# Attention in front of two expert layers: pooled v taken from 32-row blocks on TensorE, sums of outputs at the head of an iteration

## The chip, the core and the metric

The kernel runs on one core of a Trainium2 chip. TensorE (PE in the rows, its weight loads PEld) does the matmuls, VectorE (DVE), ScalarE (ACT) and GpSimd (POOL) the element work, SyncE (SP) issues the DMAs. The metric is the time of one execution on the device in microseconds (us).

## What is computed

Three layers stand behind each other: an attention, a dense layer with a gated activation, and a mixture of experts. The change touches the attention alone (batch 4, 8 heads, 576 positions, head size 64). It adds two attentions: one over positions that are averaged in fours, repeated back to full length, and a local one in which each position sees those less than four away.

```python
q_d = q.reshape(B, H, Sd, factor, D).mean(axis=3)      # factor = 4, Sd = 144
k_d = k.reshape(B, H, Sd, factor, D).mean(axis=3)
v_d = v.reshape(B, H, Sd, factor, D).mean(axis=3)
out_up = np.repeat(sm_attn(q_d, k_d, v_d), factor, axis=2)
mask = np.abs(pos[:, None] - pos[None, :]) < factor
scores = np.where(mask, scale * np.matmul(q, k.transpose(0, 1, 3, 2)), -1e9)
attn = np.exp(scores - max);  attn = attn / (sum(attn) + 1e-09)
return out_up + np.matmul(attn, v)                     # sm_attn has the same softmax
```

## The kernel before

**Units.** The attention works in 16 units u of two heads: four batches b of four pairs of heads (NP = 4). A half batch j (four heads) is loaded at once: k and q in `load_a` (tiles kn, qn, and rm for the last 64 rows). v is loaded twice. `load_v(b, n)` brings a quarter of batch b for the local attention into vw[b % 2]: 32-row blocks that overlap by eight, six blocks to a quarter, 24 to a batch, each block one DMA of 64 KB in runs of 256 bytes, for all eight heads. `load_v4(j, c)` brings the same values a second time for the pooled attention: 288 KB in runs of 1 KB, 16 such loads, which `pool_v` adds up in fours on GpSimd into vp.

**The loop.** Iteration `it` of 20 runs a pipeline over the units, each engine in program order: `transposes(it+1)` on TensorE, `copies(it+1)` and `p_copies(it+1)` on ScalarE (they bring k and q, transposed, from PSUM into SBUF), `normalize(it-1)` and `p_normalize(it-1)` (sums and reciprocals on VectorE, products on GpSimd), `merge(it-3)` (VectorE adds pooled and local outputs, SP stores them), `scores(it)` and `p_scores(it)` on TensorE, `relay(it+2)` (ScalarE and VectorE reorder k and q), `load_a`, `outputs(it-2)` on TensorE, `softmax(it)` and `p_softmax(it)` (maxima on VectorE, exponentials on ScalarE), `scatter(it-1)`, `p_transposes(it-1)`, `pt_copies(it-1)`, and then the pooling of the next half batch on GpSimd and the loads of v. Between them `prep_step` puts pieces of the preparation of the dense layer's weights (DVE lines 204, 209, 214, 219, ACT lines 195 and 199), one or two of them an iteration at first, three from iteration 5 on.

**What sets the order.** All loads go through SP's one queue in program order. Eight semaphores are used for them in turn, so that from the ninth DMA on each waits until the one eight places ahead of it has landed. PSUM has eight banks that `bank()` hands out in turn: ten to an iteration, so that each use waits for the readers of the use eight before it. The last five iterations also hold the first matmuls of the dense layer (L711). With iteration 16 the attention's own loads are over; behind the attention the program is a dense and an expert layer.

The lines of before that the steps need: transposes L381 to L383, copies L392 to L405, scores L413 and L418, pooled scores L453, softmax L426 to L428, pooled softmax L462 and L464, sums L434 to L437 and L469 to L471, scatter L443 and L447, pooled transposes and copies L479 and L486, outputs L499 to L506, merge L518, v loads L330 and L340, v pooling L354 and L355.

## Time and profile before

| | us |
|---|---|
| median of 3 runs (lowest, highest) | 845.87 (843.55, 846.75) |
| the profiled execution | 849.41 |
| its span | 847.7 |

| engine | busy us of the span |
|---|---|
| PE | 761.4 (90%) |
| DVE | 593.6 (70%) |
| ACT | 526.9 (62%) |
| POOL | 220.3 (26%) |

The span is the profiled execution without what lies around it (1.7 us). The busy shares are means over stages with different limits. From about 164 us on PE is busy for 635.97 of the 684.10 us left; the attention, which the change touches, lies ahead of that, and there no engine is busy all the time. The stretches below are cut at the starts of the mask matmul (L413) of an iteration: iteration 2 starts at 24.07, 3 at 41.37, 7 at 70.57, 14 at 129.06 us.

### The profile page before, as it was taken

What the parts mean: (1) busy time and instruction counts of PE and PEld (TensorE: products, weight loads), DVE (VectorE), ACT (ScalarE), POOL (GpSimd) and SP (SyncE); (2) the same over time, 40 slices, a digit from 0 to 9 for tenths busy, and PEclk for the clock granted to TensorE, in tenths of its full rate; (3) what the DMA queues carried; (4) which work ended last, traced back from release to release, by engine and by line L of the source; (5) the groups of instructions that cost most, each with busy time, mean ns of one, the idle gap of its engine ahead of it and who ended that gap; (6) DMA issues with size and microseconds to landing.
All of it is one profiled execution on the core that took longest, in us unless ns stands there. A gap on an engine that the chain in (4) does not pass through costs nothing. (4 is left out here: it accounts for less than half of the span.)

```text
span 847.7 us, 14454 instructions
## 1 busy us (share of the span) xinstructions
PE 761.4 (90%) x5078; PEld 644.4 (76%) x5078; DVE 593.6 (70%) x1414; ACT 526.9 (62%) x1019; POOL 220.3 (26%) x212
## 2 busy tenths in 40 slices
PE   5597786799979999999999899899789999999991
PEld 4475665588858888888899788789688887899981
DVE  6499998689966874388439658968766555666652
ACT  6597886899846556655666567554336554565551
POOL 7577673100000000000000110337323232332330
PEclk9699988999979999999999999999999999999996
DMA  7999991455623110010001004546577667767762
GB/s 171 221 185 217 233 239 62 142 149 180 192 66 127 63 26 0 14 57 20 0 13 58 20 29 183 76 39 197 103 223 222 208 194 235 223 228 240 199 213 63
DMA packets 90066, 112.99 MB, mean 133 GB/s; under 512 B 39915, under 2 KB 62077, under 8 KB 89725
## 3 DMA queue, kind: packets, MB, share of 16 engines
q1 hardware_dynamic: 85421, 101.35, 44.7%
q0 software_dynamic: 4560, 10.60, 3.6%
q8 instruction: 42, 0.69, 0.4%
q14 instruction: 43, 0.35, 0.2%
HBM read 97.06 MB, written 15.12 MB: 132 GB/s over the span
## 5 line engine op out<-in xcount | busy, mean ns | idle before, releaser
L731 DVE TENSOR_TENSOR t<-bk,t 128x512 f32<-128x512 f32 (+1 forms) x80 | 50.0, 633 | 100.8 <-ACT t L725 100.8
L678 POOL DMA_INDIRECT ids_by_expert<-tok_id,g_pi x18 | 20.8, 1154 | 279.1 <-DVE run L677 104.3
L638 DVE SCALAR_TENSOR_TENSOR junk<-o,wgb 128x512 f32<-128x512 f32 x120 | 85.0, 708 | 2.9
L719 ACT ACTIVATE t<-bk 128x512 f32<-128x512 f32 (+1 forms) x80 | 44.0, 550 | 54.5 <-PE bk L711 52.8
L740 DVE TENSOR_TENSOR gg<-t,gg 128x512 fp32r<-128x512 f32 (+1 forms) x80 | 57.3, 720 | 7.5 <-ACT gg L729 4.2
L729 ACT CAST gg<-t 128x512 fp32r<-128x512 f32 (+1 forms) x57 | 32.7, 573 | 40.0 <-DVE t L731 33.7
L711 PE MATMUL bk<-x,wi0h 128*128 128x512 f32 (+1 forms) x160 | 52.3, 407 | 5.4 <-DVE x L699 5.1
L720 ACT ACTIVATE t<-t,half 128x512 f32<-128x512 f32 (+1 forms) x80 | 54.6, 682 | 2.6
L1097 POOL DMA_INDIRECT out_dram<-yo,oid x19 | 25.4, 1338 | 115.7 <-ACT yo L1096 69.2
L1083 ACT ACTIVATE hT<-bk 128x256 fp32r<-128x256 f32 x80 | 30.4, 383 | 35.6 <-PE bk L1081 33.1
L725 ACT ACTIVATE t<-t,hpi 128x512 f32<-128x512 f32 (+1 forms) x80 | 52.2, 674 | 0.2
L711 PE MATMUL bk<-x,wi1h 128*128 128x512 f32 (+1 forms) x160 | 47.8, 381 | 4.2 <-DVE t L731 4.2
L751 PE MATMUL bk<-wo1h,gg 128*128 128x512 f32 x144 | 48.3, 406 | 0.0
L1084 DVE SCALAR_TENSOR_TENSOR hT<-bk,hT 128x256 fp32r<-128x256 f32 x80 | 32.9, 420 | 21.5 <-ACT hT L1083 21.4
L711 PE MATMUL bk<-x,wi3h 128*128 128x512 f32 (+1 forms) x160 | 46.9, 375 | 0.6 <-DVE rank L673 0.6
L711 PE MATMUL bk<-x,wi2h 128*128 128x512 f32 (+1 forms) x160 | 46.1, 369 | 0.0
L751 PE MATMUL bk<-wo3h,gg 128*128 128x512 f32 x144 | 46.1, 392 | 0.0
L751 PE MATMUL bk<-wo0h,gg 128*128 128x512 f32 x144 | 45.9, 393 | 0.0
L751 PE MATMUL bk<-wo2h,gg 128*128 128x512 f32 x144 | 45.8, 392 | 0.0
L711 PEld LDWEIGHTS bk<-x,wi0h 128*128 128x128 f32 x160 | 31.9, 204 | 13.6 <-DVE x L699 7.0
L711 PEld LDWEIGHTS bk<-x,wi1h 128*128 128x128 f32 x160 | 30.6, 195 | 8.9 <-DVE t L731 4.6
L1081 PE MATMUL bk<-x,ew10h 128*128 128x256 f32 x160 | 31.8, 288 | 5.7 <-DVE x L1016 2.4
(308 smaller groups left out, 2338.2 us busy)
## 6 DMA issues: line engine op xcount, KB each, us to landing
est<-in_moe_w_dram SPq DMA_DIRECT2D x88, 512.0 KB
wst<-in_moe_w_in_dram SPq DMA_DIRECT2D x16, 512.0 KB
wst<-in_moe_w_out_dram SPq DMA_DIRECT2D x16, 512.0 KB
vw<-in_v_dram SPq DMA_DIRECT2D x88, 64.0 KB
v<-in_v_dram SPq DMA_DIRECT2D x16, 288.0 KB
x_second<-o SPq DMA_DIRECT2D x18, 256.0 KB
kn<-in_k_dram SPq DMA_DIRECT2D x8, 512.0 KB
qn<-in_q_dram SPq DMA_DIRECT2D x8, 512.0 KB
```

The costliest lines, as they stand in the source:

```text
L638: V.scalar_tensor_tensor(wgb["junk"], x2[tl], 1.0, wgb[e], op0=ALU.mult, op1=ALU.mult, accum_out=gate[tl][:, e:e + 1])
L711: PE.matmul(h, a[:, f % QF, kk], x[:, c], start=n == 0, stop=n == 3 * KD - 1)
L719: A.activation(t, bk[f % GF][:, :BLK[j]], AF.Tanh, scale=0.5)
L720: A.activation(t, t, AF.Arctan, scale=-0.5, bias=half)
L725: A.activation(t, t, AF.Sin, scale=-2.0, bias=hpi)
L729: A.copy(gg[:, 0], t_)
L731: V.tensor_tensor(t, bk[f % GF][:, :BLK[j]], t, op=ALU.mult)
L740: V.tensor_tensor(gg[:, 1], t, gg[:, 0], op=ALU.subtract)
L751: PE.matmul(acc[t], gg[:, a, c], w[:, f % QF], start=f == 0 and n == 0, stop=f == NF - 1 and n == 2)
L1081: PE.matmul(ps[:, :256], W1(i, a, kk, f), xt[i][:, c, kk], start=n == 0, stop=n == 3 * KD - 1)
L1083: A.activation(hT[:, 0, f], ps[:, :256], AF.Relu)
L1084: V.scalar_tensor_tensor(hT[:, 1, f], ps[:, :256], 0.0, hT[:, 0, f], op0=ALU.max, op1=ALU.subtract)
```

## The change

**Pooled v.** `load_v4` and `pool_v` go. `pool_vw(b)` takes the sums from the 32-row blocks: a matrix pool_v (128 x 32, built once) with ones where a row belongs to a group of four; six matmuls of 512 columns for a batch write 32 PSUM rows each, at one of four column places of the array, into two banks; two ScalarE copies bring them to vp. This stands at the end of iterations 1, 5, 9 and 13. The 32-row layout leaves eight idle rows in each 32, so the pooled probabilities `pe` get the same layout, with zeros between (two tiles that GpSimd clears once), and their transposes and products have 128 and 64 rows in place of 72 and 72.

**Loads.** All four quarters of the first batch are loaded ahead of the loop, ahead of `load_a(2)`, which stood between the second and the third quarter. Of each later batch two quarters are loaded in iteration 4b+1, one each in the next two; before, one in each of four iterations.

**The order.** `merge(it-3)` moves from behind the sums to the head of the iteration.

**Constants.** The exponentials e get a 33rd column that holds 1e-9, so that one sum (L434) gives the denominator and L435 goes. The scaling and constant of the pooled sums moves from VectorE (L469) to ScalarE, behind the exponentials.

```diff
+    KP = (128, 32 * (T - 4))
+        es = [ac.tile([128, 2 * T, W + 1], F32, name=f"e{i}") for i in range(2)]
+        pool_v = ac.tile([128, W], F32, name="pool_v")
+        pes = [ac.tile([128, LQ, T, W], F32, name=f"pe{i}") for i in range(2)]
...
+            for t in es:
+                V.memset(t[:, :, W:], 1e-9)
...
-            for t in pbd:
+            for t in pbd + pes:
                 G.memset(t, 0.0)
...
-        def pool_v(j, c):
-            v4 = bt[j]["v4", c]
-            vp = wk.tile([HS, HB, D], F32, tag="vp", name="vp", bufs=6)
-            G.tensor_tensor(v4[:, :, 0:2], v4[:, :, 0:2], v4[:, :, 2:4], op=ALU.add)
-            G.tensor_tensor(vp, v4[:, :, 0], v4[:, :, 1], op=ALU.add)
-            bt[j]["vp", c] = vp
+        def pool_vw(b):
+
+            ps = [bank(f"pv{c}") for c in range(2)]
+            for t in range(T):
+                c, i = divmod(t, 4)
+                PE.matmul(ps[c][32 * i:32 * i + 32], pool_v, vw[b % 2][:, t], tile_position=(0, 32 * i))
+            vp = wk.tile([128, 2, H * D], F32, tag="vp", name="vp", bufs=1)
+            for c in range(2):
+                A.copy(vp[:KP[c], c], ps[c][:KP[c]])
+            st["v"] = vp
...
-            V.tensor_reduce(sm, e, axis=X, op=ALU.add)
-            V.tensor_scalar(sm, sm, 1e-9, None, op0=ALU.add)
+            V.tensor_reduce(sm, es[u % 2], axis=X, op=ALU.add)
...
-                A.activation(pe[:, g], p3[:, g], AF.Exp, bias=pm[:, g:g + 1], accum_out=pz[:, g:g + 1])
+                A.activation(pe[:, g, :, :QB], p3[:, g].rearrange("p (t a) -> p t a", t=T), AF.Exp, bias=pm[:, g:g + 1], accum_out=pz[:, g:g + 1])
+            A.activation(pz, pz, AF.Copy, scale=4.0, bias=4e-9)
...
-            V.tensor_scalar(pz, pz, 1e-9, 4.0, op0=ALU.add, op1=ALU.mult)
             V.reciprocal(pz, pz)
...
-        for c in range(2):
-            load_v4(0, c)
-        for n in range(NP - 1):
+        for n in range(NP):
             load_v(0, n)
-            if n == LA:
-                load_a(2)
+        load_a(2)
         setup_p()
...
-        pool_v(0, 0)
-        load_v4(1, 0)
...
+            if 3 <= it < U + 3:
+                merge(it - 3)
             if it + 1 < U:
                 transposes(it + 1)
...
-            if 3 <= it < U + 3:
-                merge(it - 3)
...
-            m, odd = divmod(it + 1, 2)
-            b, n = divmod(it + NP - 1, NP)
-            if b < B:
-                load_v(b, n)
-            if m < NH:
-                pool_v(m, odd)
-            if m + 1 < NH:
-                load_v4(m + 1, odd)
+            b, n = divmod(it, NP)
+            if n == 1 and b < B:
+                pool_vw(b)
+            if n and b + 1 < B:
+                for z in ((), (0, 1), (2,), (3,))[n]:
+                    load_v(b + 1, z)
```

**SP's queue ahead of the loop.** vw_169 is the buffer of batch 0, v_267 and v_269 are the second copy of v. Before:

```order
L330 DMA v_267<-in_v_dram 72x4x256
L330 DMA v_269<-in_v_dram 72x4x256
L340 DMA vw_169<-in_v_dram 28x8x64
L340 DMA vw_169<-in_v_dram 32x8x64 x11
L323 DMA kn<-in_k_dram 128x4x256
L324 DMA rm<-in_k_dram 64x4x64
L323 DMA qn<-in_q_dram 128x4x256
L324 DMA rm<-in_q_dram 64x4x64
L340 DMA vw_169<-in_v_dram 32x8x64 x6
```

and now:

```order
L344 DMA vw_169<-in_v_dram 28x8x64
L344 DMA vw_169<-in_v_dram 32x8x64 x22
L344 DMA vw_169<-in_v_dram 28x8x64
L333 DMA kn<-in_k_dram 128x4x256
L334 DMA rm<-in_k_dram 64x4x64
L333 DMA qn<-in_q_dram 128x4x256
L334 DMA rm<-in_q_dram 64x4x64
```

All 24 blocks of batch 0 stand directly behind the first two half batches of k and q; the third half batch stands behind them.

**TensorE at the end of iteration 1 and in iteration 2.** Before, the pooled transposes of unit 0 (L479) are followed by the transposes of unit 3, and v is first read by the outputs of unit 0:

```order
L479 MATMUL bk_97<-ident,pe 72x128 x2
L479 MATMUL bk_97<-ident,pe 72x32
L381 MATMUL bk_90<-ident,rl 128x128 x4
L382 MATMUL bk_92<-ident,pl 128x128
L381 MATMUL bk_91<-ident,rl 128x128 x4
L382 MATMUL bk_92<-ident,pl 128x128
L383 MATMUL bk_92<-pool_id,rm 128x2x80
L413 LDWEIGHTS id_b
L413 MATMUL bk_93<-mask,id_b 128x384
L418 MATMUL bk_93<-spare_98,qT_165 32x64 x24
L453 MATMUL bk_94<-kp,qbd_167 128x144 x3
L499 MATMUL bk_95<-pp,vp 64x144 x4
```

and now:

```order
L487 MATMUL bk_97<-ident,pe_174 64x128 x2
L487 MATMUL bk_97<-ident,pe_174 64x32
L360 MATMUL bk_90<-vw_169,pool_v 32x512 x4
L360 MATMUL bk_91<-vw_169,pool_v 32x512 x2
L389 MATMUL bk_92<-ident,rl 128x128 x4
L390 MATMUL bk_94<-ident,pl 128x128
L389 MATMUL bk_93<-ident,rl 128x128 x4
```

The six matmuls read all blocks of v, and the transposes and scores of the next units are queued behind them.

**VectorE in an iteration** (the one that holds the first weight piece, L204). Before, the merge (L518) stands between the reciprocals and the relay:

```order
L434 TENSOR_REDUCE sm<-e 128x12
L435 TENSOR_SCALAR sm<-sm 128x12
L436 RECIPROCAL sm<-sm 128x12
L469 TENSOR_SCALAR pz<-pz 128x3
L470 RECIPROCAL pz<-pz 128x3
L518 TENSOR_TENSOR x<-bk_96,pos 128x288
L518 TENSOR_TENSOR x<-bk_97,pos 128x288
L360 TENSOR_REDUCE rl<-qn 128x512
L204 TENSOR_SCALAR wm<-wm 128x512
```

and now:

```order
L526 TENSOR_TENSOR x<-bk_92,pos 128x288
L526 TENSOR_TENSOR x<-bk_93,pos 128x288
L442 TENSOR_REDUCE sm<-e_171 128x12
L443 RECIPROCAL sm<-sm 128x12
L477 RECIPROCAL pz<-pz 128x3
L368 TENSOR_REDUCE rl<-qn 128x512
L203 TENSOR_SCALAR wm<-wm 128x512
```

Two small operations are gone, and only the relay still stands between the reciprocals, which start GpSimd's products, and the weight piece.

## Rows read from the trace of the kernel before

**Rows 1.** Busy time of each engine in stretches; last PEclk, DMA share, GB/s.
```profile
24.07:41.37 17.30, 9.16 (x108) 6.75 (x105) 7.75 (x22) 8.76 (x27) 10.43 (x12) 0.65 1.12 230
41.37:70.57 29.20, 26.60 (x421) 21.12 (x420) 24.57 (x60) 26.67 (x89) 21.46 (x23) 0.92 0.96 197
70.57:129.06 58.49, 48.04 (x737) 37.84 (x735) 57.14 (x106) 50.06 (x160) 40.50 (x41) 0.91 0.96 224
129.06:163.60 34.54, 28.31 (x306) 21.59 (x303) 28.59 (x62) 23.71 (x61) 9.25 (x14) 0.90 0.29 97
```

**Rows 2.** Timeline, TensorE's outputs: start, us, instruction, idle before, releaser.
```profile
31.07 0.59 PE L504 MATMUL bk<-spare,vw 128*64 128x96 f32 x4 [3.79 <-DMA vw<-in_v_dram]
...
36.60 0.59 PE L504 MATMUL bk<-spare,vw 128*64 128x96 f32 x4 [0.93 <-DMA vw<-in_v_dram]
...
66.43 0.43 PE L504 MATMUL bk<-spare,vw 128*64 128x96 f32 x4 [2.05 <-DMA vw<-in_v_dram]
```

**Rows 3.** Timeline, ScalarE: first copy of units 3, 4 and 5.
```profile
25.33 0.58 ACT L392 COPY spare<-bk 64x512 f32<-64x512 f32 x1
...
39.80 0.58 ACT L392 COPY spare<-bk 64x512 f32<-64x512 f32 x1 [0.65 <-PE bk L381]
...
47.88 0.58 ACT L392 COPY spare<-bk 64x512 f32<-64x512 f32 x1
```

**Rows 4.** Timeline, SP's queue: issues of v, from the start on.
```profile
6.61 1.88 SPq L330 DMA_DIRECT2D v<-in_v_dram  x2
8.60 12.19 SPq L340 DMA_DIRECT2D vw<-in_v_dram  x12
...
23.35 3.06 SPq L340 DMA_DIRECT2D vw<-in_v_dram  x6
...
28.46 3.86 SPq L340 DMA_DIRECT2D vw<-in_v_dram  x6
```

**Rows 5.** Timeline, GpSimd: pooling of v.
```profile
15.44 1.26 POOL L354 TENSOR_TENSOR v<-v 72x512 f32<-72x512 f32 x1 [1.64 <-DMA v<-in_v_dram]
16.78 0.73 POOL L355 TENSOR_TENSOR vp<-v 72x256 f32<-72x256 f32 x1
```

**Rows 6.** Timeline: prices of small-tile and full fp32 matmuls, a 512-column copy, a small ScalarE operation.
```profile
18.60 0.88 PE L418 MATMUL bk<-spare,qT 128*32 128x64 f32 x48
...
19.41 1.00 PE L453 MATMUL bk<-kp,qbd 128*128 128x144 f32 x6
...
49.29 0.59 ACT L394 COPY qT<-bk 128x512 f32<-128x512 f32 x1
...
17.60 0.19 ACT L464 ACTIVATION_READ_ACCUMULATOR pe<-bk,pm 128x1 f32 x1
```

**Rows 7.** Groups of instructions from 70.57 to 129.06: count, busy, mean ns, idle before.
```profile
L428 ACT ACTIVATE e<-e 128x384 f32<-128x384 f32 x7 | 3.7, 524 | 6.3 <-DVE e L427 6.3
...
L469 DVE TENSOR_SCALAR pz<-pz 128x3 f32<-128x3 f32 x6 | 2.9, 481 | 0.0
...
L435 DVE TENSOR_SCALAR sm<-sm 128x12 f32<-128x12 f32 x6 | 1.5, 242 | 0.2
```

**Rows 8.** Timeline: weight pieces on VectorE beside GpSimd's products.
```profile
97.63 2.51 DVE L204 TENSOR_SCALAR wm<-wm 128x512 int32<-128x512 int32 x1
...
143.06 0.68 DVE L209 SCALAR_TENSOR_TENSOR wm<-wst,wm 128x512 int32<-128x512 int32 x1
...
143.12 1.39 POOL L471 TENSOR_TENSOR pe<-pe,pz 128x432 f32<-128x432 f32 x1
...
150.57 0.42 DVE L204 TENSOR_SCALAR wm<-wm 128x512 int32<-128x512 int32 x1
```

**Rows 9.** Timeline of iteration 15: the merge, and the outputs that wait for its bank.
```profile
141.16 0.55 DVE L434 TENSOR_REDUCE sm<-e 128x12 f32<-128x384 f32 x1
...
142.33 0.81 DVE L518 TENSOR_TENSOR x<-bk,pos 128x288 f32<-128x288 f32 x2
...
142.84 1.23 PE L504 MATMUL bk<-spare,vw 128*64 128x96 f32 x12 [4.83 <-DVE x L518]
```

More of the change, by code (lines that the diff above doesn't have):

```diff
@@ L158, in moe_kernel @@
     LAG = 5
-    LA = 1
     SC_A = (0, 1)
@@ L285, in setup_a @@
             V.tensor_copy(pool_id[:, :, RP:], ident[:2 * CR, :2 * CR].rearrange("p (z r) -> p z r", z=2))
+            V.memset(pool_v, 0.0)
+            V.tensor_reduce(
+                pool_v[:, :QB].rearrange("p (i a) -> p i a", i=4),
+                ident.rearrange("p (i w) -> p i w", i=4)[:, :, 4:4 + QB].rearrange("p i (a f) -> p i a f", f=4),
+                axis=X, op=ALU.add,
+            )
+            for t in es:
+                V.memset(t[:, :, W:], 1e-9)
             V.tensor_copy(id_b, ident)
@@ L325, in load_a @@
             bt[j] = {"n": (kn, qn), "rm": rm}
-        def load_v4(j, c):
-            b, h0 = j // 2, j % 2 * HB
-            v4 = ld.tile([HS, HB, 4, D], F32, tag="v4", name="v4")
-            SP.dma_start(out=v4.rearrange("p h r d -> p h (r d)"), in_=v[b, h0:h0 + HB, c * 4 * HS:(c + 1) * 4 * HS, :].rearrange("h (p r) d -> p h (r d)", r=4))
-            bt[j]["v4", c] = v4
         def load_v(b, n):
@@ L422, in softmax @@
             sc = st.pop(("s", u))
-            e = wk.tile(gsh, F32, tag="e", name="e")
+            e = es[u % 2][:, :, :W]
             mx = wk.tile([128, 2 * T], F32, tag="mx", name="mx")
@@ L442, in scatter @@
             et = wk.tile(gsh, F32, tag="et", name="et", bufs=1)
-            V.transpose(et.rearrange("p g q -> p (g q)"), e.rearrange("p g w -> p (g w)"))
+            V.transpose(et, e)
             pb = pbd[u % 2].rearrange("p t h i q -> p (t h) i q")
@@ L457, in p_softmax @@
             psc = st.pop(("ps", u))
-            pe = wk.tile([128, LQ, SPL], F32, tag="pe", name="pe")
+            pe = pes[u % 2]
             pm = wk.tile([128, LQ], F32, tag="pm", name="pm")
@@ L468, in p_normalize @@
             pe, pz = st["p", u]
-            V.tensor_scalar(pz, pz, 1e-9, 4.0, op0=ALU.add, op1=ALU.mult)
             V.reciprocal(pz, pz)
-            G.tensor_tensor(pe, pe, pz.unsqueeze(2).to_broadcast([128, LQ, SPL]), op=ALU.mult)
+            p4 = pe[:, :, :, :QB]
+            G.tensor_tensor(p4, p4, pz.unsqueeze(2).unsqueeze(3).to_broadcast([128, LQ, T, QB]), op=ALU.mult)
         def p_transposes(u):
@@ L483, in pt_copies @@
             tps = st[("q", u)]
-            pp = wk.tile([HS, 2, 2 * SPL], F32, tag="pp", name="pp", bufs=1)
+            pp = wk.tile([128, 2, 2 * SPL], F32, tag="pp", name="pp", bufs=1)
             for c in range(2):
-                A.copy(pp[:, c], tps[c][:HS, :2 * SPL])
+                A.copy(pp[:KP[c], c], tps[c][:KP[c], :2 * SPL])
             st["q", u] = pp
@@ L491, in outputs @@
             b, pg = divmod(u, NP)
-            vp, w_ = [bt[j]["vp", c] for c in range(2)], vw[b % 2]
+            vp, w_ = st["v"], vw[b % 2]
             pp = st.pop(("q", u))
@@ L498, in outputs @@
                 for h in range(2):
-                    PE.matmul(po[64 * h:64 * h + 64], vp[c][:, 2 * p + h], pp[:, c, SPL * h:SPL * h + SPL], start=c == 0, stop=c == 1, tile_position=(0, 64 * h))
+                    PE.matmul(po[64 * h:64 * h + 64], vp[:KP[c], c, (2 * pg + h) * D:(2 * pg + h + 1) * D], pp[:KP[c], c, SPL * h:SPL * h + SPL], start=c == 0, stop=c == 1, tile_position=(0, 64 * h))
             o = [bank(f"xo{i}") for i in range(2)]
```

3 lines of the change are left out of this document (1 added, 2 removed).

## Prediction, made before the changed kernel was run

> **What bounds the kernel now.** I read the stretches first [rows 1], since the busy shares of the whole span mix stages. The change lies in the first 164 us; what follows is moved as a whole, so a gain there is a gain of the run. The four stretches have different limits. From 24.07 to 41.37, iteration 2, no engine is busy for more than 10.43 of 17.30 us, while the DMA engines are full: this is a wait for loads. The timeline says which: TensorE stands three times before the outputs of unit 0, until 36.60, for blocks of v [rows 2]. From 41.37 to 70.57 ScalarE is busy for 26.67 of 29.20 us over four iterations, 6.7 us for each: it sets the pace, but for one more wait for v, 2.05 us at 66.43 [rows 2]. From 70.57 to 129.06 VectorE is busy for 57.14 of 58.49 us, and ScalarE for 50.06; ScalarE's largest wait there, 6.3 us, is for VectorE [rows 1, 7]. From 129.06 on engines wait for each other in turn; the longest such wait is TensorE's 4.83 us before 142.84 for a bank that the merge must empty [rows 9]. A gain within 0.5% (4.2 us) could not be told from no change.
>
> **The start.** On ScalarE the copies of unit 3 begin at 25.33, of unit 5 at 47.88 [rows 3]: 22.6 us for two iterations that take 13.4 at ScalarE's own pace. So 9.2 us are lost there, to v and to what follows from it (TensorE's granted clock is 0.65 of full speed in that stretch [rows 1]). Now the second copy of v is gone and all 24 blocks stand together. Before, twelve were issued in 12.19 us from 8.60 on [rows 4]; the seventh had to wait for the first of the pooled-v loads, since it stands eight places behind it, and that load had landed only when GpSimd took it at 15.44 [rows 5]. Later blocks cost SP 0.51 to 0.64 us each (3.06 and 3.86 for six [rows 4]). With the first twelve out by about 16 (14.7 at 0.51 each, 20.8 as before), the other twelve at 0.55 and some 3 us to land (before, the last left SP at 32.3 and was used at 36.60, which bounds it at 4.3), v is complete at about 25.6, and at 23 to 31 by the bounds. TensorE now needs it at the end of iteration 1 and not in iteration 2. One matmul and one copy stand behind the last block, so ScalarE begins unit 3 at about 27.1, 1.8 late, and unit 5 two iterations of 6.9 later, at 40.9 in place of 47.88: 7.0 us. The third half batch of k and q is now issued behind v, which I charge with 1. **Gain 6**, bounds 2 and 8.
>
> **The pooled v.** Six fp32 matmuls of 512 columns are 3072 columns a batch. The nearest row in form, 24 matmuls of 64 columns at the same four column places of the array, takes 0.88 us for 1536 columns [rows 6]: 1.8 us a batch. Full-width fp32 matmuls take 1.00 us for three of 144 columns [rows 6]: 7.1 us a batch, the other end. I take 1.8. The Trainium skill (TensorE: Matmul & The Clock Gate, Why this matters for your kernels) gives 2.38 times for three column tiles with 512 columns; by that figure the six would take an estimated 3.0 us, and the run would be at most 4.8 us longer. The two copies are of 512 columns, 0.59 each [rows 6]: 1.2 us of ScalarE a batch. TensorE's 1.8 hides beside the copies of the unit before where ScalarE sets the pace; if that cover is gone it costs 1.8 for each of the three later batches. The 16 poolings on GpSimd, 1.26 and 0.73 [rows 5], were off the path: they go for nothing, and in their place the clearing of the two pe tiles at the start costs nothing.
>
> **ScalarE's small operation.** It is one more small operation a unit; the read-out of a sum takes 0.19 [rows 6], so 0.2. On VectorE it and L435 took 2.9 and 1.5 us in seven iterations [rows 7]. The 33rd column, the wider transposes and the constants cost nothing that I can see: the sums grow by 3%, the rest is covered.
>
> **From 41.37 to 70.57.** ScalarE's pace stays. The 2.05 of waiting goes, since a batch is complete about two iterations before it is read; four small operations (0.8) and one pair of copies (1.2) come. **Gain 0**, bounds 2 lost (TensorE's 1.8 uncovered) and 1 won.
>
> **From 70.57 to 129.06.** VectorE goes from 57.14 to 52.7; ScalarE from 50.06, with seven small operations and two pairs of copies, to 53.9. ScalarE is late next: with no waits the stretch would be 4.6 shorter. Two engines this close do not run without waits, and ScalarE has 2.1 us of others than those for VectorE already (58.49 less 50.06 and 6.3), so I leave 3. **Gain 1.7**, bounds 2 lost and 4.6 won.
>
> **From 129.06 on.** The sum and the reciprocals of unit 14, from 141.16 to 142.33, no longer stand ahead of the merge for which TensorE waits [rows 9]. **Gain 1.2**, bounds 0.5 and 2. Elsewhere, too, the merge frees its banks sooner; SP stores its result from the same place in its queue.
>
> **The sum.** 6 + 0 + 1.7 + 1.2 = 8.9 us. The profiled execution would go from 849.4 to 840.5; the median of the runs, 3.5 lower than it, from 845.9 to **837.0**.
>
> **The rivals.** *VectorE loses a cover.* The merge (0.81 [rows 9]) ran beside GpSimd's first product. Now the weight pieces come that much sooner, under the products. A piece of 0.42 took 2.51 at 97.63, but one that came just before the end of a product, at 143.06, took 0.68 and GpSimd's next took 1.39 [rows 8]. If every piece waits the cover out, seven iterations lose 0.81 each, 5.7 in all, and the run is at 842.7: no difference that could be told. The Trainium skill (SBUF — State Buffer, SBUF: two separate sides) has a rule that speaks for this: one port pair is shared by VectorE and GpSimd, whoever starts first keeps it for the whole instruction, and the other is blocked. By that rule the trace agrees at 97.63, and 143.06 shows that the wait also ends with one product. For it: from iteration 5 on three weight pieces fall in an iteration, two of them right behind the relay. Against it: one pooling of v fewer in each iteration stands in the way, and ScalarE, not VectorE, is then late. *TensorE is held.* The six matmuls stand ahead of all transposes and scores; if they are dear, or wait for the last block in each of four batches, X us each beyond 1.8, the run is at 837.0 + 4X. From X = 3.3 on it is slower than 850.1; at 7.1 a batch (X = 5.3) it is 858, at X = 4 it is 853. For it: all blocks are needed an iteration sooner, and 64 KB loads with eight in flight were slow at the start. Against it: from the second batch on the last quarter is issued two iterations ahead, 13 us, and the row of the same form is cheap. *All packs well.* The start at its bound of 8, ScalarE at its floor (4.6), the tail at 2: 14.6, and 831.3. *The pooling saves nothing, as it was hidden anyway,* holds for GpSimd's part and is in the sum.
>
> **How the numbers follow.** The forecast, 833 to 841.6: 0.52. All packs well, below 833: 0.15. Cover lost, 841.6 to 850: 0.21. TensorE held, above 850.1: 0.12. So faster 0.67, same 0.21, slower 0.12. The range of 830 to 846 leaves out about 0.04 below and 0.16 above.
>
> **What would show it.** In the profile after, TensorE's waits for v before the outputs are gone, and one of about 3 us stands before the first pooling matmul, near 22; the copies of unit 5 begin near 41; the six matmuls take about 1.8 us; from iteration 7 on ScalarE is busy for nearly all of the stretch, and VectorE waits for it. A start that gains less than 3 us, weight pieces of over 1.5 us in every iteration, or a wait for v before each batch's pooling would make the prediction wrong.

## The result: 832.5 us where 837.0 was predicted

The changed kernel takes **832.48 us** (median of 4 runs, 831.81 to 833.77), the kernel before beside it 846.31 us; the ratio is **0.9863, 95% interval 0.9832 to 0.9894**. The forecast was 837.0, in a range of 830 to 846, with a chance of 0.67 for faster. The sign and the range held. The time is 4.5 us below the forecast and falls, by half a microsecond, into the case "all packs well" (below 833, chance 0.15) and not into the forecast's own 833 to 841.6. The experiments show that one of the reasons given was wrong, and that pooling v on TensorE gained only through the loads that it made needless.

The profiled execution of the changed kernel took 831.83 us, with a span of 829.7. Its stretches, at the same places of the program as [rows 1] (from the mask matmul of one unit to that of another); after the length come PE, PEld, DVE, ACT and POOL busy, then TensorE's granted clock as a share, the DMA share and GB/s:

```profile
28.39:34.83 6.44, 6.44 (x107) 4.87 (x105) 4.48 (x11) 5.80 (x21) 4.69 (x6) 1.00 1.12 294
34.83:63.58 28.75, 28.01 (x434) 20.00 (x432) 22.51 (x57) 28.14 (x96) 15.50 (x18) 1.00 0.74 174
63.58:117.64 54.06, 50.82 (x761) 36.23 (x759) 47.29 (x99) 52.49 (x173) 26.55 (x26) 0.97 0.75 193
117.64:154.16 36.52, 28.31 (x306) 20.63 (x303) 26.79 (x52) 28.14 (x69) 7.73 (x12) 0.95 0.35 113
```

Unit 3 begins at 34.83 in place of 41.37: 6.5 us. Iterations 3 to 7 take 28.75 in place of 29.20, iterations 7 to 14 take 54.06 in place of 58.49: 0.4 and 4.4 us. I take the first multiplication of the dense part on VectorE for the end of attention: it came at 167.1 before and comes at 154.2, so the rest gave 1.5. A second profile of the kernel before, taken later, has the stretches 28.63 and 58.12 and the end at 165.7; differences of some 0.5 us in a stretch, and of 1.5 at the end, mean nothing. Iterations 3 to 7 scatter by more: they take 27.0 to 29.2 us in the four profiles below that have the loads of the kernel before. Behind attention, the dense part lasts 403.7 us before and 402.0 after. The last part, the experts, lasts 276.9 and 273.5 in these two profiles, 272.3 in the second one of before, and between 263 and 274 in the runs below (e1 and e3 apart, whose experts do other work): it scatters by more than most of the edits are worth. So I judge edits by their stretches of attention first, and by the time only where its interval is narrow enough. One execution of e4, of 1389 us, was in the slow state and is left out of its median.

TensorE's pooling matmuls (timeline: start, us, instruction, idle before, releaser):

```profile
22.15 1.90 PE L360 MATMUL bk<-vw,pool_v 128*32 128x512 f32 x10
...
26.02 1.02 PE L360 MATMUL bk<-vw,pool_v 128*32 128x512 f32 x2 [1.97 <-DMA vw<-in_v_dram]
...
53.38 1.91 PE L360 MATMUL bk<-vw,pool_v 128*32 128x512 f32 x12
...
82.70 1.91 PE L360 MATMUL bk<-vw,pool_v 128*32 128x512 f32 x12
...
114.26 1.91 PE L360 MATMUL bk<-vw,pool_v 128*32 128x512 f32 x12
```

There is one wait for a block of v, 1.97 us, before the last matmul of the first batch, and none later; TensorE's waits before the outputs [rows 2] are gone. SP's queue (timeline) issues all 24 blocks of the first batch in one row, where the first twelve alone took 12.19 us [rows 4]:

```profile
7.88 14.73 SPq L344 DMA_DIRECT2D vw<-in_v_dram  x24
22.71 0.39 SPq L333 DMA_DIRECT2D kn<-in_k_dram  x1
```

ScalarE's first copies of units 3, 4 and 5 (timeline), to be read against 25.33, 39.80 and 47.88 [rows 3]:

```profile
27.66 0.58 ACT L400 COPY spare<-bk 64x512 f32<-64x512 f32 x1
...
35.40 0.59 ACT L400 COPY spare<-bk 64x512 f32<-64x512 f32 x1
...
42.19 0.58 ACT L400 COPY spare<-bk 64x512 f32<-64x512 f32 x1
```

And four groups of VectorE's and one of GpSimd's from 63.58 to 117.64 (count, busy us, mean ns, idle before):

```profile
L213 DVE SCALAR_TENSOR_TENSOR wm<-wst,wm 128x512 int32<-128x512 int32 x5 | 4.1, 820 | 0.0
...
L434 DVE TENSOR_REDUCE mx<-bk 128x12 f32<-128x384 f32 x7 | 3.9, 552 | 2.8 <-PE bk L426 2.8
L208 DVE SCALAR_TENSOR_TENSOR wm<-wst,wm 128x512 int32<-128x512 int32 x4 | 3.8, 944 | 0.0
L203 DVE TENSOR_SCALAR wm<-wm 128x512 int32<-128x512 int32 x5 | 3.1, 628 | 0.0
...
L479 POOL TENSOR_TENSOR pe<-pe,pz 128x432 f32<-128x432 f32 x7 | 8.7, 1247 | 0.0
```

The first weight piece and the pooled product in the same stretch before:

```profile
L204 DVE TENSOR_SCALAR wm<-wm 128x512 int32<-128x512 int32 x5 | 8.8, 1754 | 0.0
...
L471 POOL TENSOR_TENSOR pe<-pe,pz 128x432 f32<-128x432 f32 x7 | 6.3, 906 | 0.4 <-DVE pz L470 0.4
```

Here is the surprise. The first weight piece takes 628 ns on average; in the same stretch before, the five of them took 1754 on average. VectorE's busy time fell by 9.85 us (57.14 to 47.29), while the two operations that left it had 4.4 [rows 7]. And GpSimd's product of the pooled softmax, 906 ns before, takes 1247 now.

### The profile page after: what moved, and what is told of

Its sections match the earlier page's. It is cut to its first block, busy times and chain, and to the rows that moved or that the text cites. A ratio compares the mean times of both kernels' runs of the same rounds, so it can differ in the third digit from the quotient of the medians.

```text
span 829.7 us, 14465 instructions
## 1 busy us (share of the span) xinstructions
PE 764.8 (92%) x5126; PEld 638.4 (77%) x5126; DVE 576.2 (69%) x1386; ACT 531.5 (64%) x1043; POOL 192.7 (23%) x182
## 4 chain that ended last, share of the span: by engine, by line
PE 48%; DVE 14%; ACT 13%; DMA 11%; issue 8%; POOL 2%; SPq 2%; POOLq 0%; ACTq 0%
PE bk L712 17%; PE bk L752 15%; PE bk L1082 5%; DVE junk L639 4%; DMA est<-in_moe_w_dram 3%; PE bk L1093 3%; DMA tid<-ids_by_expert,ridx 3%; DMA out_dram<-yo,oid 2%; DVE t L732 2%; ACT pe L471 1%; DVE gg L741 1%; DMA xg<-x_second,tid 1%; ACT wm L198 1%; ACT t L721 1%; PE bk L512 1%
## 5 line engine op out<-in xcount | busy, mean ns | idle before, releaser
L994 POOL DMA_INDIRECT xg<-x_second,tid x22 | 25.2, 1147 | 42.6 <-DMA tid<-ids_by_expert,ridx 17.2
```

## The experiments

All twelve, in stretches of their profiles (us; "unit 3" is the start of its mask matmul, "end" the end of attention as above), and in time. Each ratio is to executions of the kernel before that ran beside that run (their medians lie between 842.4 and 846.3), so it is not the quotient of two medians of this table. A profile is one execution; those of e2, e4 and e5 are the fastest of their runs.

| run | unit 3 | 3 to 7 | 7 to 14 | end | median | ratio to before (95%) |
|---|---|---|---|---|---|---|
| before, first profile | 41.37 | 29.20 | 58.49 | 167.1 | 846.31 | |
| before again (e12) | 41.82 | 28.63 | 58.12 | 165.7 | 843.43 | 1.0014 (0.9977, 1.0051) |
| changed | 34.83 | 28.75 | 54.06 | 154.2 | 832.48 | 0.9863 (0.9832, 0.9894) |
| e1 pooling only | 34.60 | 33.32 | 62.02 | 168.1 | 941.2 | not comparable |
| e2 constants only | 40.85 | 27.02 | 58.73 | 163.7 | 844.44 | 0.9986 (0.9960, 1.0012) |
| e3 add moved back | 34.98 | 33.61 | 63.06 | 170.7 | 943.83 | not comparable |
| e4 GpSimd's additions back | 36.70 | 28.83 | 55.45 | 157.5 | 830.82 | 0.9854 (0.9808, 0.9900) |
| e5 second copy loaded again | 37.62 | 34.58 | 63.37 | 172.0 | 847.16 | 1.0057 (1.0032, 1.0083) |
| e6 both back | 43.81 | 30.16 | 63.88 | 174.2 | 849.49 | 1.0077 (1.0051, 1.0103) |
| e7 add back in 3 of 4 | 34.82 | 28.73 | 54.37 | 155.3 | 832.83 | 0.9884 (0.9841, 0.9926) |
| e8 add moved, alone | 41.03 | 27.73 | 58.29 | 164.8 | 838.12 | 0.9944 (0.9912, 0.9977) |
| e9 before, no second copy | 33.07 | 26.36 | 53.44 | 150.9 | 829.72 (one run) | not comparable |
| e10 second copy, other queue | 38.66 | 30.72 | 65.47 | 171.3 | 838.77 | 0.9951 (0.9928, 0.9974) |
| e11 a copy moved to GpSimd | 33.79 | 27.35 | 54.18 | 151.3 | 828.37 | 0.9838 (0.9789, 0.9887) |

### Which of the three edits

The theory at this point, P: the pooling of v, with the loads and GpSimd's work that it does away with, carries nearly all. The rivals: the small operations that left VectorE (C), or the earlier add of the outputs (M).

**e1** undoes the constants and the place of the add, **e3** the place of the add alone. The edit of e3, which e1 has too:

```diff
-            if 3 <= it < U + 3:
-                merge(it - 3)
             if it + 1 < U:
                 transposes(it + 1)
...
                 p_normalize(it - 1)
+            if 3 <= it < U + 3:
+                merge(it - 3)
```

> The changed kernel with two of its three edits undone: outputs are added up behind normalize again, and the constant of the local sums and the scaling of the pooled sums are VectorE's small operations again. What is left is v pooled on TensorE. Theory P (the pooling carries nearly the whole gain: start by the loads of the second copy, iterations 7 to 14 by GpSimd's freed share of memory): mask matmul of unit 3 within 0.5 us of the changed kernel's 34.8, iterations 7 to 14 at 54.5 to 55.5 us (54.06 changed, 58.49 before), time 833 to 835 us. Rival C (the two small edits give the gain of iterations 7 to 14): the start as changed, but iterations 7 to 14 at 57 to 58.5 us, time 836 to 838 us.

> The changed kernel with one edit undone: outputs are added up behind normalize, as before. Theory P: no more than 0.5 us in iterations 7 to 14 (54.06 us changed), time within 1 us of the changed kernel's 832.5. Rival M (the earlier add frees the bank and the copies sooner, and that is why ScalarE packs): iterations 7 to 14 at 55.5 to 57 us, time 834 to 836 us. Below zero is possible for both: the add stands ahead of the copies of the next unit in the changed kernel, 0.4 us each time, so undoing it could also give 1 us back.

Neither did what it was meant to do. The pooled v takes two more banks in every fourth iteration. Counted from the outputs of a unit, the third bank of the next transposes is then the outputs' own first one again, and with the add behind the transposes the outputs of one unit in four are overwritten before they are added. The router sees other numbers and sends tokens elsewhere, so the times of 941 and 944 us say nothing. What TensorE and VectorE wait for in e3's iterations 7 to 14 (waits: us in total, times, longest) shows the same loop from the other side:

```profile
PE bk L421 <- DVE x L526: 8.8, 2, 4.6
```

```profile
DVE x L526 <- ACT qbd L413: 8.9, 2, 4.9
```

The add waits for the copies out of the new transposes, and the mask matmul for the add; the iterations behind a pooling last 12 to 13 us where the changed kernel has 8.2. So the add at the head is no refinement: it is what makes room for the two banks. It can be undone in three iterations of four, and alone on the kernel before:

**e7** leaves the add at the head in the iterations behind a pooling and puts it back elsewhere (`it % NP == 2` at the head, the others behind normalize). **e8** moves it on the kernel before. **e2** makes the edit of the constants on the kernel before:

```diff
-            V.tensor_reduce(sm, e, axis=X, op=ALU.add)
-            V.tensor_scalar(sm, sm, 1e-9, None, op0=ALU.add)
+            V.tensor_reduce(sm, es[u % 2], axis=X, op=ALU.add)
...
+            A.activation(pz, pz, AF.Copy, scale=4.0, bias=4e-9)
...
-            V.tensor_scalar(pz, pz, 1e-9, 4.0, op0=ALU.add, op1=ALU.mult)
```

> The changed kernel with the add of the outputs put back behind normalize in three of four iterations; in the fourth, behind the one that pools v, it stays at the head, since the two banks of the pooled v bring the rotation of banks round to the outputs before they are added. Nothing is left out of the computation. Theory P: the place of the add is worth at most 0.5 us in iterations 7 to 14 (54.06), time 832 to 833.5 us. Rival M: the earlier add is what lets ScalarE pack, 55.5 to 57 us and 834 to 836 us.

> The kernel before with only the add of the outputs moved to the head of the iteration. Theory P: within 0.7 us in every stretch (start 41.4, iterations 7 to 14 at 58.49), time 845.5 to 847 us; VectorE does the add 0.45 us a piece before the work that follows, where it waits for weight pieces anyway. Rival M: iterations 7 to 14 at 55.5 to 57 us, time 843 to 844.5 us.

> The kernel before with only the edit of the constants: 33rd column in the local sums, scaling of the pooled sums on ScalarE. GpSimd still pools v, the second copy of v is still loaded. Theory P: iterations 7 to 14 lose at most 1 us of 58.49, the start does not move (unit 3's mask matmul at 41.4 plus or minus 0.5), time 845 to 846.5 us where the kernel before has 846.3. Rival C: iterations 7 to 14 lose 2 to 4 us, time 842 to 844 us.

e7 is the changed kernel within 0.4 us in both stretches, and its time cannot be told from the changed kernel's. e8 leaves iterations 7 to 14 at 58.29: rival M falls. But the profile of e8 shows more than that. Its stretch (columns as in the first fence), its first weight piece, GpSimd's product, and what VectorE waits for:

```profile
68.76:127.05 58.29, 48.06 (x737) 38.17 (x735) 51.19 (x115) 50.11 (x162) 42.65 (x42) 0.91 1.03 233
...
L204 DVE TENSOR_SCALAR wm<-wm 128x512 int32<-128x512 int32 x5 | 3.3, 666 | 0.0
...
L471 POOL TENSOR_TENSOR pe<-pe,pz 128x432 f32<-128x432 f32 x7 | 8.7, 1239 | 0.0
...
DVE x L518 <- DMA x_t<-x: 5.7, 2, 3.0
```

The second copy is still loaded here, GpSimd still adds it up and waits 7.0 us for it, and yet the piece is as short as in the changed kernel, the product as long, and VectorE is busy for 51.19 us in place of 57.14. So the place of the add alone does to these instructions what I called the surprise. The stretch is no shorter for it: VectorE now waits 5.7 us for stores of x (in part perhaps because the add comes earlier; no run separates that). e7 says the same from the other side: with the add put back in three iterations of four VectorE is busy for 51.59 us where the changed kernel has 47.29, the product is at 932 ns, and the stretch is 54.37 against 54.06. In both kernels VectorE's busy time changes by 4 to 6 us and the length does not follow.

In time e8 is 4.8 us below the kernel before (ratio 0.9944), more than the 0.9 to 2.3 us by which attention ends earlier. Its dense part took 401.6 us where both profiles of the kernel before have 403.6 and 403.7; its last part took 272.9, between their 272.3 and 276.9, so the profiles do not place the rest of the gap. Why it is there stays open. e2 leaves iterations 7 to 14 at 58.73: rival C falls, and with it a step of the prediction (below). VectorE's groups in that stretch of e2 show where the room went:

```profile
L204 DVE TENSOR_SCALAR wm<-wm 128x512 int32<-128x512 int32 x5 | 9.2, 1837 | 0.0
L214 DVE SCALAR_TENSOR_TENSOR wm<-wst,wm 128x512 int32<-128x512 int32 x4 | 7.5, 1877 | 0.0
```

The two groups had 8.8 and 5.0 us in the first profile of the kernel before (7.7 and 6.9 in the second). The operations went, the pieces behind them took longer by 2.9 us (2.1), and VectorE's busy time is 57.26 us instead of 57.14 (56.67).

### Loads or additions

**e4** puts GpSimd's additions back into the changed kernel, on tiles that nothing loads. **e5** puts the loads of the second copy back at their old places, into tiles that nobody reads. **e6** has both: each pair of additions waits for its load, as before.

```diff
+            G.tensor_tensor(v4[:, :, 0:2], v4[:, :, 0:2], v4[:, :, 2:4], op=ALU.add)
+            G.tensor_tensor(dp, v4[:, :, 0], v4[:, :, 1], op=ALU.add)
...
+            SP.dma_start(out=dv[c].rearrange("p h r d -> p h (r d)"), in_=v[b, h0:h0 + HB, c * 288:(c + 1) * 288, :].rearrange("h (p r) d -> p h (r d)", r=4))
```

> The changed kernel with GpSimd's two additions of each half of v put back at their old places, on a tile of zeros that nothing loads and nobody reads. Loads stay as changed. Theory P: the start stays within 0.7 us (unit 3's mask matmul at 34.8), VectorE's int32 weight pieces are longer again (628 to 944 ns each changed, 820 to 1754 before), and iterations 7 to 14 go from 54.06 to 55.5 to 58 us, time 834 to 837 us. Rival C (VectorE's removed operations gave it): pieces longer but iterations 7 to 14 within 0.7 us of 54.06, time within 1 us of 832.5.

> The changed kernel with the loads of the second copy of v put back at their old places in SP's order (two ahead of the first quarter of v, then one in each iteration), into tiles that nobody reads. GpSimd pools no v. Theory L (the second copy holds the start): unit 3's mask matmul goes from 34.8 back to 38.5 to 41.4 us, time plus 4 to 6 us, 837 to 839. Rival S (the start moved because nothing of the start waits for GpSimd's pooling any more): within 0.7 us of 34.8. For iterations 7 to 14 (54.06 changed, 58.49 before): theory W, that GpSimd's pooling waits for its load there and pushes GpSimd's other work onto VectorE's weight pieces, expects 54 to 55 us here and int32 pieces of some 630 ns; rival D, that the transfers themselves make VectorE's pieces long, expects 56.5 us and more and pieces of 1200 ns and more.

> Both put back: the loads of the second copy of v at their old places, and GpSimd's additions of each half at theirs, which wait for them. Their sums are read by nobody; v is pooled on TensorE as changed. Theory W: VectorE's first int32 piece from some 630 ns to over 1200 ns and iterations 7 to 14 at 57 to 58.5 us, though the pooling alone (no loads) left the pieces at 627 ns and the iterations at 55.45; unit 3's mask matmul at 39 to 41.4; time 840 to 845 us. Rival D: as the run with the loads alone, within 0.7 us in each stretch. Rival C (the three small operations that left VectorE): pieces long, but iterations 7 to 14 at most 56 us.

e4: GpSimd is busy 41.16 us in iterations 7 to 14, as much as before (40.50), and VectorE's first piece does not mind:

```profile
L203 DVE TENSOR_SCALAR wm<-wm 128x512 int32<-128x512 int32 x5 | 3.1, 627 | 0.0
```

The stretch is 1.4 us longer, unit 3 is 1.9 later (two more tiles are cleared at the start, to which I put it down without a run of its own), and the time is that of the changed kernel. The amount of GpSimd's work alone is not what stretched VectorE's pieces; the half of P that put the gain there falls. Rival C, which expected longer pieces and the length of the changed kernel, fits no better.

e5: the loads alone, read by nobody, take the whole gain away, and more: 14.7 us by the medians, some 16 by the two ratios. I had expected 4 to 6, all at the start. But unit 3 loses only 2.8, and iterations 3 to 7 and 7 to 14 lose 5.8 and 9.3. None of the four theories had that: the start lies between L and S, and the stretch is long, as rival D asked, but with pieces that stay short. What VectorE waits for in iterations 7 to 14 of e5 (waits), and its first piece there:

```profile
DVE x L533 <- DMA x_t<-x: 9.4, 3, 4.7
DVE x L533 <- PE bk L433: 4.3, 1, 4.3
...
L203 DVE TENSOR_SCALAR wm<-wm 128x512 int32<-128x512 int32 x5 | 3.7, 745 | 0.0
```

and TensorE's pooling matmuls of the third batch (timeline):

```profile
93.31 1.06 PE L367 MATMUL bk<-vw,pool_v 128*32 128x512 f32 x8
...
96.46 3.08 PE L367 MATMUL bk<-vw,pool_v 128*32 128x512 f32 x4 [2.09 <-DMA vw<-in_v_dram]
```

The add writes into one of two tiles and has to wait until the store of two units ago has read it; the store is late, I take it because the transfers ahead of it in SP's queue are. And the pooling waits for the last blocks of its batch, with all of TensorE's transposes and scores behind it. This is the rival *TensorE is held*, and its condition: it comes when the second copy is still loaded.

e6: here the start is lost too (unit 3 at 43.81), by another road. GpSimd's and TensorE's rows (two timelines of e6):

```profile
35.71 1.26 POOL L285 TENSOR_TENSOR dv<-dv 72x512 f32<-72x512 f32 x1 [3.04 <-DMA dv<-in_v_dram]
37.05 0.72 POOL L286 TENSOR_TENSOR dp<-dv 72x256 f32<-72x256 f32 x1
37.73 0.83 POOL L457 TENSOR_TENSOR e<-e,sm 128x384 f32<-128x384 f32 x1
38.52 0.90 POOL L492 TENSOR_TENSOR pe<-pe,pz 128x432 f32<-128x432 f32 x1
```

```profile
39.48 1.68 PE L500 MATMUL bk<-ident,pe 128*128 128x128 f32 x6 [3.57 <-POOL pe L492]
```

GpSimd's additions wait for their load, the products of the softmax are queued behind them, and TensorE waits for the products. Before, the same queue stood still for 4.53 us until 31.92, and the product came at

```profile
34.72 0.90 POOL L471 TENSOR_TENSOR pe<-pe,pz 128x432 f32<-128x432 f32 x1
```

so it was done at 35.62, one microsecond before TensorE's last wait for v ended at 36.60 [rows 2]. In the kernel before this road lay just behind that of v's blocks. The first int32 piece of e6 in iterations 7 to 14:

```profile
L203 DVE TENSOR_SCALAR wm<-wm 128x512 int32<-128x512 int32 x5 | 6.0, 1195 | 0.0
```

It takes almost twice as long as in the changed kernel, just under what theory W (GpSimd's wait for its load pushes GpSimd's other work onto VectorE's pieces) asked. But iterations 7 to 14 of e5 and e6 are alike (63.37 and 63.88), the waits for the stores being in both: beside the loads, GpSimd's wait and the longer pieces cost 0.5 us there, no more than the scatter. What the copy costs in the kernel before takes the reverse experiment.

### Take the second copy from the kernel before

**e9** is the kernel before with one thing taken away, the loads of the second copy (two tiles, cleared once by VectorE, stand in for them). Everything else is old: additions on GpSimd, small operations on VectorE, the add behind normalize.

```diff
-            v4 = ld.tile([HS, HB, 4, D], F32, tag="v4", name="v4")
-            SP.dma_start(out=v4.rearrange("p h r d -> p h (r d)"), in_=v[b, h0:h0 + HB, c * 4 * HS:(c + 1) * 4 * HS, :].rearrange("h (p r) d -> p h (r d)", r=4))
+            v4 = dv[c]
```

> The kernel before without the loads of the second copy of v: GpSimd makes its additions at their places on tiles of zeros, so the pooled v is zero, the router sends tokens elsewhere, and only the stretches of attention can be compared. Theory W (GpSimd's wait for that copy, with the normalization queued behind it, is what the kernel before paid in iterations 7 to 14 and in half of the start): iterations 7 to 14 at 54.5 to 56 us (58.49 before, 54.06 changed), VectorE's first int32 piece under 900 ns (1754 before), unit 3's mask matmul at 35 to 38 (41.37 before). Rival T (the 15 us of additions themselves, wherever they fall, hold VectorE): iterations 7 to 14 at 57 to 58.5 us and the pieces over 1300 ns, the start as in theory W.

Its stretches of iterations 3 to 7 and 7 to 14, in the columns of the first fence:

```profile
33.07:59.43 26.36, 24.94 (x423) 19.62 (x420) 23.80 (x64) 25.91 (x89) 22.82 (x26) 1.00 0.78 175
59.43:112.87 53.44, 45.59 (x737) 35.52 (x735) 50.79 (x108) 50.15 (x163) 39.70 (x39) 0.97 0.85 202
```

This settles which of the parts carries the gain. Without the copy the old kernel goes through iterations 7 to 14 in 53.44 us, a little faster than the changed one (54.06), with GpSimd's 39.70 us of work and VectorE's small operations still there. It starts unit 3 at 33.07 and ends attention at 150.9, 3.3 us *ahead* of the changed kernel. Rival T falls, and theory W's ranges for the stretch and for the start lie above what was measured. The groups of VectorE in iterations 7 to 14 of e9:

```profile
L204 DVE TENSOR_SCALAR wm<-wm 128x512 int32<-128x512 int32 x5 | 4.5, 890 | 0.0
...
L437 DVE TENSOR_SCALAR sm<-sm 128x12 f32<-128x12 f32 x6 | 1.2, 194 | 0.2
...
L471 DVE TENSOR_SCALAR pz<-pz 128x3 f32<-128x3 f32 x6 | 0.8, 126 | 0.1
```

The pieces are at half their length (1754 before), and the operation on 128x3, for which [rows 7] has 2.9 us, costs 0.8. The rest of the 2.9 was waiting. The kernel before, on GpSimd around 95 (timeline), shows what for:

```profile
94.89 1.26 POOL L354 TENSOR_TENSOR v<-v 72x512 f32<-72x512 f32 x1 [3.73 <-DMA v<-in_v_dram]
96.23 0.72 POOL L355 TENSOR_TENSOR vp<-v 72x256 f32<-72x256 f32 x1
96.92 0.83 POOL L437 TENSOR_TENSOR e<-e,sm 128x384 f32<-128x384 f32 x1
97.71 0.91 POOL L471 TENSOR_TENSOR pe<-pe,pz 128x432 f32<-128x432 f32 x1
98.57 1.28 POOL L347 TENSOR_TENSOR h<-qn 128x512 f32<-128x512 f32 x1
```

GpSimd stands for 3.73 us, until a half of v has landed, and then runs without a gap. So its work falls together with VectorE's: the piece that needed 2.51 us at 97.63 [rows 8] lies under the last two of these rows and the addition behind them. That explains the long piece, but not the long stretch. In e8 GpSimd waits as long at the same place, 3.91 us until 94.20, the piece at 97.53, with the add no longer ahead of it, takes 0.53 us, and the stretch takes as long as before.

What does go with the length is the copy. The four profiles of the kernel before and its variants that load it (before, e12, e2, e8) take 58.1 to 58.7 us, with a DMA share of 0.96 to 1.03 (the view's figure, which can pass 1); e9 takes 53.44, with 0.85. Through which waits the transfers hold the stretch is not shown: GpSimd's for v (6.0 to 7.3 us in those four), the stores of x (5.7 in e8), or TensorE's granted clock, which is 0.91 in all four and 0.97 in e9.

### Queue or bytes

**e10** is e5 with the loads of the second copy issued on GpSimd's queue in place of SP's (`G.dma_start` for `SP.dma_start`).

> As the run with the loads alone (the changed kernel plus the loads of the second copy of v, read by nobody: 847.2 us, iterations 7 to 14 at 63.37), but those loads are issued on GpSimd's queue in place of SP's. Theory Q (what they cost is their place in SP's queue, ahead of the windowed v and of the stores of x): iterations 7 to 14 at 54 to 56 us, unit 3's mask matmul within 1 us of 34.8, time 833 to 837 us. Rival B (the bytes cost it, 4.7 MB more through the same DMA engines): iterations 7 to 14 at 60 us or more, time 843 us or more.

Iterations 7 to 14 last 65.47 us: it is the bytes (sixteen loads of 288 KB, 4.7 MB), not their place in SP's queue. VectorE's waits in that stretch:

```profile
DVE x L533 <- DMA x_t<-x: 14.4, 4, 5.1
```

SP then issues twelve blocks of v in 9.21 us (at 64.99) where the changed kernel's SP needs 7.30 for the corresponding twelve (at 58.79), and the stores of x stand behind them. The issuing does not hold up GpSimd, whose waits in that stretch name VectorE alone. The time, though, was 838.8 us and not 843 or more, with attention ending at 171.3, as in e5 (172.0). The dense parts are alike (401.9 and 402.0 us); the last part took 263.0 in the profile of e10 and 267.2 in that of e5, and by the medians the gap is 8 us (9 by the ratios). No run here says why, so this stays open: the mechanism in attention is rival B's, the total fits neither.

### Another engine for one copy

**e11** is a try at a faster kernel: GpSimd, idle for half of iterations 7 to 14, takes the copy of k into head order.

```diff
-                (copy_1 if len(out) else A.copy)(t, n[:, 2 * p:2 * p + 2].rearrange("p h r d -> p r h d"))
+                (copy_1 if len(out) else G.tensor_copy)(t, n[:, 2 * p:2 * p + 2].rearrange("p h r d -> p r h d"))
```

> The changed kernel with one of ScalarE's copies moved to GpSimd: the copy of each unit's k into head order ahead of its transposes, 0.62 us each, 16 in all. Theory S (in the changed kernel ScalarE's own 52.49 us set the 54.06 of iterations 7 to 14): they come to 50.5 to 52.5 us, iterations 3 to 7, where TensorE is busy 28.01 of 28.75, stay within 0.5 us, time 828 to 831 us. Rival V (GpSimd's copies, longer than ScalarE's, keep VectorE's pieces waiting, or the transposes wait for them): iterations 7 to 14 at 54 us or more, time 832 us or more.

```profile
33.79:61.14 27.35, 27.35 (x434) 20.04 (x432) 21.70 (x55) 26.53 (x93) 17.20 (x21) 1.00 0.80 177
61.14:115.32 54.18, 50.39 (x762) 34.99 (x759) 47.96 (x99) 49.77 (x167) 31.10 (x33) 1.00 0.78 194
```

The time is the lowest here, 828.4 us, and attention ends at 151.3. It beats the kernel before; that it beats the changed one (ratio 0.9838 against 0.9863, with intervals that overlap) is likely from the 2.9 us in attention and not shown by the times. The reason was wrong: the gain is at the start (1.0), in iterations 3 to 7 (1.4), where none was expected, and behind iteration 14 (0.6), and iterations 7 to 14 stayed at 54.18 although ScalarE's work there fell to 49.77. What holds them now was not tried. TensorE is busy for 50.39 us, and three of the seven iterations are long: 9.9 and 8.4 us with a pooling in them and 9.7 without one, where the other four take 6.4 to 6.7.

### How far the stretches repeat

**e12** is the kernel before, unchanged.

> The kernel before, unchanged, once more, for its stretches in a second profiled execution. The runs with one small edit each on the kernel before reached the end of attention at 163.7 us (constants) and 164.8 us (add moved) where the profile of the kernel before has 167.1. If the stretches repeat (theory R): unit 3 at 41.4, iterations 3 to 7 at 29.2, 7 to 14 at 58.5, end at 166.6 to 167.6 us, each within 0.5 us, and the 3.4 and 2.3 us are the edits'. If they scatter (rival N): iterations 3 to 7 at 27 to 28 us with a granted clock near 1, the end at 164 to 166 us, and those two edits gave no more than 1 us each in attention.

Something between the two: 28.63 and 58.12, the end at 165.7. The 2.0 us of e2 and the 0.9 us of e8 that remain against it are at the edge of what a profile can tell; neither theory R nor rival N had all its ranges met. What it shows better is how VectorE's groups vary in one and the same kernel, in the same stretch:

```profile
L214 DVE SCALAR_TENSOR_TENSOR wm<-wst,wm 128x512 int32<-128x512 int32 x4 | 6.9, 1735 | 0.0
...
L469 DVE TENSOR_SCALAR pz<-pz 128x3 f32<-128x3 f32 x7 | 1.6, 231 | 0.0
```

In the first profile the first was 1248 ns and the second 481 ns [rows 7]: the wait lands on one instruction or on another, and the sum for VectorE stays (57.14 and 56.67).

## Why the prediction was right, point by point

**The start: right in size, and in mechanism for the kernel before, with a second road missed.** Forecast 6 us, measured 6.5. In its steps: v complete at 25.6, and the last pooling matmuls began at 26.02; a wait of about 3, and it was 1.97; ScalarE at unit 3 at 27.1, and it was 27.66; at unit 5 at 40.9, and it was 42.19. The wait stood before the sixth matmul and not, as forecast, before the first. What the prediction did not see is the second road by which the copy can hold the start, GpSimd's queue: with the loads alone unit 3 is at 37.62, with loads and additions at 43.81. Before, the product on that road was done at 35.62, so by these rows v alone, made earlier, would have brought little. That the change takes GpSimd's wait away too is luck, as far as the forecast goes.

**The pooling matmuls: right.** 1.8 us a batch was taken, 1.91 measured, with no wait in the three later batches. The other end, 7.1, was far off. The estimate of 3.0 worked out from the Trainium skill (TensorE: Matmul & The Clock Gate, Why this matters for your kernels) does not hold for these twelve matmuls.

**Iterations 3 to 7: right in the sum, with one limit missed.** Forecast 0, measured 0.4 (0.1 lost against the second profile). e9 separates what went and what came: without the copy the old kernel takes 26.36 us, 2.3 to 2.8 less than before, where the forecast had 2.05; the changed kernel's 28.75 give 2.4 of it back, where the forecast had 2.0. With the scatter of this stretch the sizes are rough. The prediction gave the pace to ScalarE alone, though [rows 1] has TensorE at 26.60 us beside ScalarE's 26.67. In the changed kernel ScalarE is busy for 28.14 and TensorE for 28.01 of the 28.75 us, so neither's new work has cover; e11 takes 1.6 us from ScalarE and the stretch falls to 27.35, for all of which TensorE is busy.

**Iterations 7 to 14: the step that failed.** Forecast 1.7 (4.6 less 3 is 1.6), measured 4.4 (4.1 against the second profile). The prediction took VectorE, busy for 57.14 of 58.49 us, for what sets the length, let it go "from 57.14 to 52.7" by the 4.4 us of two small operations, and then left 3 us of waits on ScalarE. As a sum this ended 2.8 us too high: ScalarE was busy for 52.49 us and not 53.9, as the last pair of copies came at 117.78, behind the end of the stretch, and its waits were 1.6 and not 3. The step that failed stands ahead of the sum. VectorE's busy time did not set the length: e8 has it at 51.19 us and the stretch at 58.29, and e2, without the operations, at 57.26 and 58.73. And the copy, which the prediction charged to the start and to one wait of 2.05 us, was put at nothing here, where e9 gains 5.1 us (4.7 against the second profile) by taking it away and nothing else. One error was to read an instruction's duration as its work: the 481 ns of an operation on 128x3 were mostly a wait, and a wait does not leave with the instruction that shows it. The other was to look for a wait for loads only where all engines stand idle. [rows 1] has the DMA engines busy for 0.96 of this stretch, and the group of GpSimd's additions in the kernel before has, in the last column, its idle time and the cause:

```profile
L354 POOL TENSOR_TENSOR v<-v 72x512 f32<-72x512 f32 x7 | 9.3, 1332 | 6.2 <-DMA v<-in_v_dram 6.0
```

GpSimd waits 6.0 us for v there, with the products queued behind. The prediction set GpSimd's additions at nothing, as off the path. That is right for the additions (e4); their wait showed that the loads were late.

**From 129.06 on: right.** Forecast 1.2, measured 1.5 against the first profile and 0.6 against the second.

**The sum.** 8.9 forecast, 12.9 at the end of attention (11.5 against the second profile); of the 4 us between, 2.7 are iterations 7 to 14. The rest is the start, iterations 3 to 7 and the tail, each within its bounds. Of the signs that the forecast named, ScalarE was busy for nearly all of iterations 7 to 14, but VectorE's largest wait there, 2.8 us, is for TensorE.

**The rivals.** *VectorE loses a cover* came out the other way round. The pieces do come sooner with the add moved, but they get shorter by it (666 ns in e8, 628 in the changed kernel), and GpSimd's product is the one that waits (1239 and 1247 ns on average, where one of e6's rows above has 0.90 us for the same product). The Trainium skill (SBUF — State Buffer, SBUF: two separate sides) says that whichever of VectorE and GpSimd starts first keeps the shared port pair for its whole instruction; it says this of VectorE's instructions that use both ports or read two inputs from SBUF. The runs agree in that the wait changes sides with the order of arrival; for such a rule the amount of GpSimd's work decides less than its phase, which is the kernel before against e8. The same section says that engines and DMA do not hold up one another at SBUF, and here the trace agrees as well: with the loads back but no additions (e5, e10) the first piece takes 745 and 750 ns, far from 1754. *TensorE is held* did not come either, and e5 shows that it was close to: had the second copy stayed, the run would have been 847.2, slower than before. *All packs well* is near to what happened (12.9 us at the end of attention, where it had 14.6), by a mechanism that the prediction did not have.

**Of the change itself:** what gained is that 4.7 MB are no longer loaded. What came with it, the pooling on TensorE with its copies and its wider layout, is the price of that, some 2.4 us in iterations 3 to 7 and some 3 to the end of attention against e9. The move of the add is needed for the banks; by time it gives 0.56% on the kernel before (e8), which the stretches of attention do not account for, and e7 is too wide to say whether it does so in the changed kernel. The edit of the constants is worth nothing that these runs can measure (0.9986, 0.9960 to 1.0012).

## What to carry to other kernels

Where an operation looks too long for its size (here 481 ns for three columns), compare it with the same operation elsewhere before you count it as a saving: the difference is a wait, and it moves to the next instruction. An engine that is busy for nearly all of a stretch need not set its length, since waits inside its instructions count as busy; here VectorE lost 6 of its 57 us and the stretch stayed (e8). A wait of an engine that is far from busy still counts if work for the busy engines is queued behind it (the start of e6); look at what such an engine waits for, not at its share. And data loaded twice costs more than its own transfer: it delays the stores and loads behind it, and each of these may hold an engine.

## What the runs showed of the hardware

Not expected: the same GpSimd work, with the same loads and much the same waits for them, stretches VectorE's first int32 piece to 1754 and 1542 ns on average in one order (two profiles of the kernel before) and leaves it at 666 in another (e8, where only the add of the outputs stands elsewhere), while GpSimd's product goes from 906 to 1239 ns. VectorE's reductions and its transposition keep their means in all of these (545 and 568 or 569 ns). Twelve fp32 matmuls of 32 columns of weights and 512 columns of data, at four places of the array, take 1.91 us together. And loads of 4.7 MB that nobody reads cost 14.7 us by the medians when issued on SP's queue (e5), 6.3 when issued on GpSimd's (e10: 838.8 against 832.5; some 16 and 7 by the ratios), though attention loses the same 17 to 18 us in both profiles; the difference lies behind attention and is not explained.
